# Four units in the first MLP step of a chunked mLSTM kernel, with the opening's instructions in a written order

## The chip, the cores and the metric

The kernel runs on one core of a Trainium2 chip. The core has a matrix engine (PE, with its weight loads shown as PEld), three engines for elementwise work (DVE, ACT, POOL) and SyncE (SP), which here only issues loads. Each engine runs its own instructions in the order in which they stand and waits on semaphores for the others. The metric is the device time of one execution in microseconds; lower is better. Before the change it is 519.04 us, the median of 3 runs (517.11 to 520.46).

## What is computed

An mLSTM layer (a linear recurrence with exponential gates), then an MLP on its output:

```python
for t in range(S):                       # B, H, S, D = 4, 8, 768, 40
    m_new = np.maximum(f[t] + m, i[t])
    f_stab, i_stab = np.exp(f[t] + m - m_new), np.exp(i[t] - m_new)
    C = f_stab * C + i_stab * outer(v[t], k[t])      # per head, 40 x 40
    n = f_stab * n + i_stab * k[t]
    y[t] = sigmoid(o[t]) * (C @ q[t]) / max(|n . q[t]|, 1)
x = y as [3072, 320]
h = x @ w_in                             # 320 -> 2048
out = (h * sigmoid(h)) @ w_out           # 2048 -> 320
```

The weights `w_in` and `w_out` arrive as 64-bit floats; the kernel builds 32-bit floats from their two words.

## The kernel before

The sequence is cut into chunks of 128 steps. A *unit* is one chunk of one batch entry with its 8 heads: 24 units of 128 tokens, unit n being chunk n // 4 of batch entry n % 4. Within a chunk the recurrence is attention with a decay matrix; from one chunk to the next a state `Cm` is carried. A unit passes through these stages (methods of `Unit`):

- loads: `load_qk` (q and k), `load_kvo` (k, v and the output gate), `load_d` (the decay logs, broadcast from a DRAM scratch `LFd`), `load_q`;
- the decay matrix `D`: `exps` on ACT, `mask` on POOL. For units 0 to 2 the logs come over PE instead of by a load: `spread` (tile `pd`), four matmuls for half a unit;
- `products` (PE, scores `ps`), `weigh` (DVE, scores times decay, and the column `vw` for the state), `values` (PE, `po`), `state` (PE, `pu`), `gate` (DVE, normalising and gating into `x`), `carry` (DVE and POOL, `Cm`);
- `xpose` (PE, transposes `x` into `px`), `xhi` (ACT) and `xlo` (DVE), which split the transposed result into a rounded part and a remainder, `xh` and `xl`.

The gates are scans over time on DVE, for 32 rows (batch entries times heads): `gates_scan`, `gates_sub`, `gates_sum`, `gates_top`, then `gates_flip` transposes on PE and `gates_out` stores to `LFd`. Chunk 0 is done first, the other five chunks in one piece in slots 0 to 2 of step 0.

The weights come in 18 parts (`Part`): `i0` to `i7` (256 columns of `w_in`, 256 of its rows), `c0` and `c4` (the last 64 rows for 1024 columns) and `o0` to `o7` (256 rows of `w_out`). A part is loaded (`load`), its magnitude made on ACT (`mag`), its sign and low bits joined by three DVE operations (`join`), and parts of `w_in` are split into `wh` and `wl` (`top` on ACT, `rest` on DVE).

The MLP runs in 8 *steps* of 3 units (384 tokens), each step in 16 *slots* (`fc`, 128 hidden columns). A slot has the first product `mm1` (8 matmuls into a bank `ph`), `glu` (tanh on ACT, then DVE), `halves` (split of the result into two parts, ACT and DVE, from step 1 on) and the second product `mm2` of the slot two earlier (banks `pout`). In step 0 `mm2` takes each product in full 32-bit precision, two matmul records per unit; from step 1 on three matmuls of rounded parts per unit, for which `split_out` splits one part of `w_out` in each of step 1's slots 0 to 7.

Everything is in program order: a list of calls makes the opening (units 0 to 2, parts `i0`, `c0`, `i1`, `o0`), with `spin(k)` putting k idle matmuls (tile `idle`) on PE between them; then step 0's slots carry the attention of units 3 to 5, the remaining weights and late gates by a table `extra`; from step 1 on `piece` spreads each unit's attention over 5 slots (unit 6 begins at slot 0 of step 1) and the loads for a unit two ahead. Buffers come from pools that hand them out in turn: `pb` (10 large ones, for weights, scores' operands and `xh`, `xl`), `pw` (3), and PSUM banks `psO` (3), `psH` (2), `psA` (3).

## Time and profile before

| | |
|---|---|
| median of 3 runs | 519.04 us (517.11 to 520.46) |
| the profiled execution, its own time | 517.62 us |
| its span, first to last instruction | 515.5 us |
| busy: PE, DVE, ACT, POOL | 498.8, 343.7, 267.9, 103.3 us |
| mean granted clock of PE | 0.967 |
| first MLP matmul | 47.67 us |
| first instruction of step 1 (scores of unit 6) | 121.68 us |

All durations are from the one profiled execution. PE's busy time includes idle matmuls (69 records) and, where the clock is below 1, slower matmuls; matmul records overlap, so what a group costs is read from start to start, or from the chain of waits. In a timeline row, the bracket holds the idle time of the engine ahead of it and what ended it. A row of a stretch gives each engine's busy time in it, then PE's granted clock as a share of full speed.

### The profile page before, as it was taken

The page shows a single profiled execution, that of the slowest core. Times are in us where ns is not written, and L with a number is a line of the kernel's source. Part 1 is how long each engine was busy: PE and PEld are TensorE (multiplying, and loading weights), DVE is VectorE, ACT ScalarE, POOL GpSimd, SP SyncE. Part 2 cuts the span into 40 slices and gives each one's busy share as a digit, 9 for nine tenths or more (in the row PEclk, how much of TensorE's full clock was granted, in tenths as well). Part 3 has the DMA queues.
Part 4 walks back from the last instruction along what each step waited for, and adds up shares of the span by engine and source line. Part 5 has one row for each costly group of instructions (what it writes and reads, how often), then busy time and mean ns, then how long its engine had stood idle before and what let it go on. Part 6 is the DMA issues. An engine that isn't in the chain of part 4 may idle for free.

```text
span 515.5 us, 8739 instructions
## 1 busy us (share of the span) xinstructions
PE 498.8 (97%) x3191; PEld 469.0 (91%) x3191; DVE 343.7 (67%) x664; ACT 267.9 (52%) x644; POOL 103.3 (20%) x142
## 2 busy tenths in 40 slices
PE   8899698999999999999999999999999999999996
PEld 4766677888999999999899999999899999999996
DVE  3765869995788767777677767776676666444332
ACT  2433154663665565656556566565655664334332
POOL 1110013330414313321332232233131010000000
PEclk9569698999999999999999999999999999999999
DMA  8861199880633644663464366346346210001001
GB/s 185 276 199 40 51 280 304 264 231 5 178 80 113 185 117 119 174 182 76 152 187 101 113 183 165 90 129 186 101 127 181 67 40 1 0 1 39 0 1 38
DMA packets 38496, 63.96 MB, mean 124 GB/s; under 512 B 3505, under 2 KB 16375, under 8 KB 38455
## 3 DMA queue, kind: packets, MB, share of 16 engines
q1 hardware_dynamic: 34951, 59.38, 41.5%
q10 hardware_dynamic: 3504, 4.03, 2.2%
q8 instruction: 25, 0.41, 0.3%
q14 instruction: 16, 0.13, 0.1%
HBM read 59.37 MB, written 4.03 MB: 123 GB/s over the span
## 4 chain that ended last, share of the span: by engine, by line
PE 82%; DVE 6%; DMA 5%; ACT 4%; issue 2%; SPq 1%; ACTq 1%; DVEq 0%
PE ph L615 31%; PE pout L655 29%; PE po L494 9%; PE ps L460 4%; PE idle L688 2%; PE po L485 2%; PE pu L526 2%; DMA raw<-in_qk_dram 2%; DMA wro<-in_w_out_dram 2%; ACT ob L672 1%; PE px L568 1%; DVE st L376 1%; ACT D L417 1%; DMA qt<-in_qp_dram 1%; DVE th L623 1%
## 5 line engine op out<-in xcount | busy, mean ns | idle before, releaser
L615 PE MATMUL ph<-xh,wh 128*128 128x384 f32 x384 | 138.2, 360 | 0.6 <-ACT xh L580 0.6
L615 PE MATMUL ph<-xl,wh 128*128 128x384 f32 x384 | 130.7, 340 | 0.2 <-DVE xl L586 0.2
L621 ACT ACTIVATE th<-ph 128x384 f32<-128x384 f32 x128 | 62.4, 488 | 113.9 <-PE ph L615 112.3
L655 PE MATMUL pout<-woh,gh 128*128 128x320 f32 x336 | 106.0, 316 | 1.6 <-ACT ob L672 1.0
L635 DVE TENSOR_TENSOR gl<-th,gh 128x384 fp32r<-128x384 f32 x112 | 63.1, 563 | 66.4 <-ACT gh L634 66.4
L655 PE MATMUL pout<-wol,gh 128*128 128x320 f32 x336 | 103.9, 309 | 0.0
L655 PE MATMUL pout<-woh,gl 128*128 128x320 f32 x336 | 103.7, 308 | 0.0
L634 ACT CAST gh<-th 128x384 fp32r<-128x384 f32 x112 | 57.2, 511 | 79.6 <-DVE th L623 79.5
L623 DVE SCALAR_TENSOR_TENSOR th<-th,ph 128x384 f32<-128x384 f32 x112 | 61.4, 548 | 41.8 <-ACT th L621 41.7
L615 PE MATMUL ph<-xh,wl 128*128 128x384 f32 x256 | 87.2, 340 | 0.0
L615 PEld LDWEIGHTS ph<-xh,wh 128*128 128x128 f32 x384 | 73.2, 191 | 2.5 <-ACT xh L580 0.8
L615 PEld LDWEIGHTS ph<-xl,wh 128*128 128x128 f32 x384 | 73.1, 190 | 0.9 <-DVE xl L586 0.4
L655 PEld LDWEIGHTS pout<-woh,gh 128*128 128x128 f32 x336 | 63.0, 188 | 4.2 <-ACT ob L672 4.1
L655 PEld LDWEIGHTS pout<-woh,gl 128*128 128x128 f32 x336 | 63.1, 188 | 0.0
L655 PEld LDWEIGHTS pout<-wol,gh 128*128 128x128 f32 x336 | 63.1, 188 | 0.0
L494 PE MATMUL po<-kvo,D 128*128 128x41 f32 x384 | 51.1, 297 | 6.4 <-issue 4.1
L376 DVE TENSOR_TENSOR st<-raw,st 40x512 fp32r<-40x512 f32 x64 | 52.9, 826 | 6.5 <-ACT st L374 4.6
L494 PEld LDWEIGHTS po<-kvo,D 128*128 128x128 f32 x384 | 49.9, 209 | 7.3 <-issue 4.4
L417 ACT ACTIVATE D<-D,aT 128x128 f32<-128x128 f32 x168 | 53.5, 391 | 0.5
L615 PEld LDWEIGHTS ph<-xh,wl 128*128 128x128 f32 x256 | 48.7, 190 | 0.3 <-DVE wl L246 0.3
L403 POOL TENSOR_SCALAR_AFFINE_SELECT D<-D 128x512 f32<-128x512 f32 x48 | 37.7, 805 | 55.2 <-DMA D<-LFd 32.7
L562 POOL TENSOR_TENSOR Cm<-Cm,ut 120x246 f32<-120x246 f32 (+1 forms) x32 | 22.9, 737 | 95.7 <-DVE ut L561 95.7
(82 smaller groups left out, 572.6 us busy)
## 6 DMA issues: line engine op xcount, KB each, us to landing
raw<-in_qk_dram SPq DMA_DIRECT2D x32, 480.0 KB
kvo<-in_kvo_dram SPq DMA_DIRECT2D x24, 484.0 KB
D<-LFd SPq DMA_DIRECT2D x42, 256.0 KB
wro<-in_w_out_dram SPq DMA_DIRECT2D x8, 640.0 KB
wri<-in_w_in_dram SPq DMA_DIRECT2D x8, 512.0 KB
out_dram<-ob ACTq DMA_DIRECT2D x24, 160.0 KB
qt<-in_qp_dram SPq DMA_DIRECT2D x20, 180.0 KB
lq<-LFd SPq DMA_DIRECT2D x60, 60.0 KB
```

Of the source, the lines that this page charges most:

```text
L376: nc.vector.tensor_tensor(out=t[r0 : r0 + D, :], in0=raw[r0 : r0 + D, :], in1=t[r0 : r0 + D, :].bitcast(F32), op=ALU.subtract,)
L403: nc.gpsimd.affine_select(out=d, in_=d, compare_op=ALU.is_ge, fill=fill, base=0, pattern=[[0, HH], [1, L]], channel_multiplier=-1,)
L417: nc.scalar.activation(d[:, h, :], e[:, h, :], AF.Exp, bias=aT[:, self.c, r + h : r + h + 1])
L460: nc.tensor.matmul(self.ps[hf][:, j, :], k_[:, cs], q_[:, cs], start=True, stop=True)
L494: nc.tensor.matmul(po[:, h, :], self.Dm[:, h, :], self.vt[:, h, :], start=first, stop=(h == H - 1))
L562: nc.gpsimd.tensor_tensor(out=v, in0=v, in1=tv, op=ALU.add)
L615: nc.tensor.matmul(ph, w, x, start=(i == 0), stop=(i == len(ops) - 1))
L621: nc.scalar.activation(th, ph, AF.Tanh, scale=0.5)
L623: nc.vector.scalar_tensor_tensor(out=g, in0=th, scalar=1.0, in1=ph, op0=ALU.add, op1=ALU.mult)
L634: nc.scalar.copy(gh, g)
L635: nc.vector.tensor_tensor(out=gl, in0=g, in1=gh.bitcast(F32), op=ALU.subtract)
L655: nc.tensor.matmul(self.po[t], g[:, ts], w, start=(fc == 0 and i == 0), stop=(last and i == len(ops) - 1),)
```

## The change

1. Step 0 has 4 units (512 tokens), steps 1 to 6 have 3, and step 7 has 2. Units 0 to 3 get their decay logs by `spread`.
2. In step 0 (`Opening`), hidden columns 0 to 3 are done in two halves, kind A for units 0 and 1 and kind B for units 2 and 3 (256 columns wide), and columns 4 to 15 for all four units together (kind J, 512 wide). The second products of the fourth unit lie in the free ends of the banks of units 0 and 1, as 192 and 128 columns.
3. From the first gate scan up to the end of the opening all work follows one written list, `ORDER`, word by word: `mJ4` is the first product of kind J for column 4, `a`, `b`, `n` its tanh, `glu` and second product; `p3` the scores of unit 3, `v`, `w`, `o`, `g`, `u`, `c`, `x`, `h`, `y` its further stages; `Li1`, `Mi1`, `Si1`, `Zi1`, `Ji1`, `Ti1`, `Ri1` the load, magnitude, three joins, `top` and `rest` of part `i1`; `z` one idle matmul, of which there are 30. The list ends with units 0 to 6 done and step 0 complete but for the second products of columns 14 and 15. From step 1 on the old scheme runs, starting with unit 7 (`DONE` 7).
4. Gates: chunks 0, 1 and 2 each in a piece of its own, all within the list; chunks 3 to 5 (`gates_late`) in slots 1 to 7 of step 1.
5. The five pools above become rings: a buffer is given back at a place in the program, and the next taker gets the one that was given back first.

```diff
+NW = 4 * L
+WIDE = 4
-NSTEP = NU // UPS
+NSTEP = 1 + -(-(NU - WIDE) // UPS)
-DONE = 6
+DONE = 7
+ORDER = """
+gs0 qk0 gs1 z gu1 z*5 gs2 gu0 gm0 gt0 z*2 gm1 two z Li0 z Mi0 z Lc0 z*3 p0 gf0 z s0.1 s2.1
+Si0 qk1 z Zi0 e0.1 s0.0 e0.0 Mc0 s1.0 Ji0 e1.0 z k0.1 z*2 s1.1 k0.0 kvo0 Sc0 gt1 r0 Zc0
...
+"""
+    class Ring:
+        def take(self, name, shape, dtype=F32):
+            self.held[name] = k = self.free.popleft()
+            return self.pool.tile(shape, dtype, tag=f"s{k}", name=name)
+        def give(self, *names):
+            for name in names:
+                self.free.append(self.held.pop(name))
...
+    class Opening:
+        SIDE = {"A": (0, 2), "B": (2, 4), "J": (0, 4)}
+        CUT = 512 - DM
+        def mm1(self, kind, fc):
+            u0, u1 = self.SIDE[kind]
+            ph = psH.take(f"ph0{kind}{fc}", [128, 512])[:, : (u1 - u0) * L]
+            first_product(ph, fc, xh0, xl0, slice(u0 * L, u1 * L))
...
+        def mm2(self, kind, fc):
...
+                if u < 3:
+                    nc.tensor.matmul(self.po[u][:, :DM], gs, w, start=(fc == 0), stop=last)
+                else:
+                    nc.tensor.matmul(self.po[0][:, DM:], gs, w[:, :cut], start=False, stop=False)
+                    nc.tensor.matmul(
+                        self.po[1][:, DM : 2 * DM - cut], gs, w[:, cut:], start=False, stop=False
+                    )
...
     class Step:
...
+            self.n0 = WIDE + (j - 1) * UPS
+            self.n = min(UPS, NU - self.n0)
+            self.w = self.n * L
...
+    late = gates_late()
+    rest = (3, NC - 3)
+    extra = {
+        1: dict(end=[lambda: late.scan(*rest)]),
+        3: dict(end=[lambda: late.sub(*rest)]),
+        5: dict(middle=[lambda: late.sum(*rest)], end=[lambda: late.store(*rest)]),
+        7: dict(middle=[lambda: late.top(*rest)],
+                end=[lambda: late.flip(*rest), lambda: big.give("lfi", "lml")]),
+    }
```

Three places show how instructions move. First PE, ahead of the first MLP matmul. Before (`px` are the transposes of a unit, `pu2` unit 2's state product, `ph0_0` the first product of column 0), the rows from unit 1's transposes on, the run of eleven idle matmuls shortened to its first:

```order
L568 MATMUL px1_400<-ident_83,x1_360 128x128 x2
L570 MATMUL px1_400<-ident_83,x1_360 64x128
L571 MATMUL px1_400<-ident_83,x1_360 64x128
L688 LDWEIGHTS G_97
L688 MATMUL idle_110<-G_97 128x512
...
L526 MATMUL pu2_431<-vw2_351,kvo2_161 120x123 x2
L526 MATMUL pu2_431<-vw2_351,kvo2_161 80x82
...
L568 MATMUL px2_436<-ident_83,x2_416 128x128 x2
L570 MATMUL px2_436<-ident_83,x2_416 64x128
L571 MATMUL px2_436<-ident_83,x2_416 64x128
L615 MATMUL ph0_0_486<-xh0_327,wh_89 128x384
```

Now (`ph0A0` is the first product of column 0 for units 0 and 1, `pd3_1` half of unit 3's spread):

```order
L696 MATMUL px1_366<-ident_83,x1_332 128x128 x2
L698 MATMUL px1_366<-ident_83,x1_332 64x128
L699 MATMUL px1_366<-ident_83,x1_332 64x128
L884 LDWEIGHTS G_98
L884 MATMUL idle_116<-G_98 128x512
L491 MATMUL pd3_1_379<-rows_99 128x128 x4
L653 MATMUL pu2_384<-vw2_372,kvo2_324 120x123 x2
L653 MATMUL pu2_384<-vw2_372,kvo2_324 80x82
L653 MATMUL pu1_390<-vw1_322,kvo1_285 120x123 x2
L653 MATMUL pu1_390<-vw1_322,kvo1_285 80x82
L725 MATMUL ph0A0_396<-X_97,wh_89 128x256 x2
...
L620 MATMUL po2_416<-kvo2_324,D2_172 128x41 x8
```

The first product follows unit 1's transposes, with half the width, and unit 2's values (`po2`) come behind it. Where the dots stand are the other six matmuls of `ph0A0`.

Second SP, the loads at the start (`raw` is q and k of a unit, `kvo` its k, v and gate, `wr` a weight part). Before:

```order
L334 DMA raw0_127<-in_qk_dram 40x2x512 x2
L185 DMA wri0_130<-in_w_in_dram 128x2x512
L188 DMA wrc0_132<-in_w_in_dram 64x2x512 x2
L345 DMA kvo0_135<-in_kvo_dram 128x968
L334 DMA raw1_137<-in_qk_dram 40x2x512 x2
L345 DMA kvo1_140<-in_kvo_dram 128x968
L107 DMA LFd_101<-G_97 32x128
L107 DMA LFd_101<-G_97 1x128
L334 DMA raw2_156<-in_qk_dram 40x2x512 x2
L185 DMA wri1_159<-in_w_in_dram 128x2x512
```

Now:

```order
L418 DMA raw0_112<-in_qk_dram 40x2x512 x2
L271 DMA wri0_139<-in_w_in_dram 128x2x512
L274 DMA wrc0_145<-in_w_in_dram 64x2x512 x2
L418 DMA raw1_178<-in_qk_dram 40x2x512 x2
L429 DMA kvo0_219<-in_kvo_dram 128x968
L927 DMA bm_88<-in_bmask_dram 120x123
L429 DMA kvo1_285<-in_kvo_dram 128x968
L271 DMA wri1_294<-in_w_in_dram 128x2x512
L418 DMA raw2_310<-in_qk_dram 40x2x512 x2
L429 DMA kvo2_324<-in_kvo_dram 128x968
```

Unit 1's q and k stand ahead of unit 0's `kvo`, and the gates' store to `LFd` is no longer among these; it follows the load of `kvo3`, for chunk 1 in place of chunk 0.

Third DVE, in the middle of step 0. Before, around the `glu` (L623) of columns 3 to 5:

```order
L623 SCALAR_TENSOR_TENSOR g0_3_638<-th0_3_636,ph0_3_619 128x384
L212 TENSOR_SCALAR wti3_645<-wti3_645 128x512
L215 SCALAR_TENSOR_TENSOR wti3_645<-wri3_589,wti3_645 128x512
L221 SCALAR_TENSOR_TENSOR wti3_645<-wri3_589,wti3_645 128x512
L623 SCALAR_TENSOR_TENSOR g0_4_673<-th0_4_671,ph0_4_659 128x384
L246 TENSOR_TENSOR wl_90<-wti3_645,wh_89 128x2x256
L212 TENSOR_SCALAR wto3_683<-wto3_683 128x640
L215 SCALAR_TENSOR_TENSOR wto3_683<-wro3_640,wto3_683 128x640
L221 SCALAR_TENSOR_TENSOR wo3_698<-wro3_640,wto3_683 128x640
L623 SCALAR_TENSOR_TENSOR g0_5_707<-th0_5_705,ph0_5_689 128x384
```

Now, around the `glu` (L760) of column 4, kind J (`vw4` is unit 4's column for the state, `D4` its weighted scores):

```order
L760 SCALAR_TENSOR_TENSOR g0J4_726<-g0J4_726,ph0J4_702 128x512
L294 TENSOR_SCALAR wti4_697<-wti4_697 128x512
L294 TENSOR_SCALAR wto3_730<-wto3_730 128x640
L301 SCALAR_TENSOR_TENSOR wti4_697<-wri4_538,wti4_697 128x512
L301 SCALAR_TENSOR_TENSOR wto3_730<-wro3_558,wto3_730 128x640
L599 TENSOR_TENSOR D4_495<-ps4_1_571,D4_495 128x512
L314 SCALAR_TENSOR_TENSOR wti4_697<-wri4_538,wti4_697 128x512
L314 SCALAR_TENSOR_TENSOR wo3_795<-wro3_558,wto3_730 128x640
L343 TENSOR_TENSOR wl_90<-wti4_697,wh_89 128x2x256
L294 TENSOR_SCALAR wtc4_782<-wtc4_782 128x512
```

The single operations of two parts and of a unit alternate, and the parts stand further ahead of the columns that use them: `i4` (columns 8 and 9) is joined right behind the `glu` of column 4.

More of the change, by code (lines that the diff above doesn't have):

```diff
@@ L34 @@
 NWT = 3
-DONE = 6
+DONE = 7
+CUT = 10
 TWICE = 2 * UPS
@@ L676, in mlstm_mlp_kernel @@
+            put(n, [(slice(0, DM), self.po[t])], ob)
+            psO.give(f"pout{self.j}_{t}")
+            if not own:
+                big.give(f"ob{n}")
     units = [Unit(n) for n in range(NU)]
     steps = {}
-    def load(n):
-        units[n].load_qk()
-        units[n].load_kvo()
-        units[n].load_d()
-    idle = psH.tile([128, 512], F32, tag="h", name="idle")
+    idle = []
     def spin(k):
+        if not idle:
+            idle.append(psH.take("idle", [128, 512]))
         for _ in range(k):
@@ new lines, in mlstm_mlp_kernel @@
+    UNIT = dict(qk="load_qk", kvo="load_kvo", d="load_d", q="load_q", s="spread", e="shape",
+                k="tri", p="products", v="column", w="weight", t="opened", l="scaled",
+                r="keep", o="values", g="gate", u="state", c="carry", x="xpose", h="xhi", y="xlo")
+    PART = {a + b: f for a, f in dict(
+        L="load", M="mag", S="shift", Z="signs", J="lows", T="top", R="rest").items() for b in "cio"}
+    GATE = dict(gs="scan", gu="sub", gm="sum", gt="top", gf="flip", go="store")
@@ L802, in run @@
+    MLP = {a + b: f for a, f in dict(m="mm1", a="tanh", b="glu", n="mm2").items() for b in "ABJ"}
+    OTHER = dict(z=lambda: spin(1), two=gates_two,
+                 bm=lambda: nc.sync.dma_start(bm, bmask))
+    nc.vector.memset(busy, 1.0)
+    perform(ORDER)
     def run(*calls):
```

675 lines of the change are left out of this document (344 added, 331 removed).

## The prediction

> **What bounds the kernel now.** I read the page's head, then a table of stretches cut where the program changes character: 47.67 us is the first MLP matmul, 121.68 us the start of step 1, and the last row holds slots near the end that have no attention in them.
>
> ```profile
> span 515.5 us, 8739 instructions
> ...
> 0.00:47.67 47.67, 43.25 (x224) 28.81 (x224) 24.48 (x52) 15.22 (x41) 7.08 (x18) 0.79 0.66 189
> 47.67:121.68 74.01, 67.50 (x359) 56.53 (x359) 63.80 (x114) 35.00 (x83) 15.70 (x19) 0.91 0.68 198
> 66.60:121.68 55.08, 52.81 (x288) 43.79 (x287) 47.21 (x83) 28.46 (x67) 14.10 (x17) 0.97 0.84 244
> 121.68:150.00 28.32, 28.32 (x201) 26.93 (x201) 19.77 (x36) 18.20 (x43) 7.13 (x9) 1.00 0.31 85
> 455.02:507.36 52.34, 52.19 (x325) 51.82 (x325) 21.17 (x38) 20.29 (x41) 0.00 (x0) 1.00 0.03 10
> ```
>
> The columns are window, its length, then busy us of PE, PE's weight loads, DVE, ACT and POOL, the granted clock, DMA share and GB/s. From 121.68 us on PE is full at clock 1.00: there the time is the sum of PE's work, and nothing but less work shortens it. Ahead of it PE reads as busy too, but at a clock of 0.79 and 0.91, and partly with idle matmuls. DVE, the next busiest, works 24.48 of the first 47.67 us and 63.80 of the next 74.01.
>
> Next the timeline of PE: where it stood still, and the two marks.
>
> ```profile
> 14.15 0.79 PE L460 MATMUL ps<-raw 40*128 40x128 f32 x2 [1.95 <-DMA raw<-in_qk_dram]
> 47.67 0.44 PE L615 MATMUL ph<-xh,wh 128*128 128x384 f32 x1 [0.57 <-ACT xh L580]
> 56.52 3.61 PE L494 MATMUL po<-kvo,D 128*128 128x41 f32 x16 [4.08 <-issue]
> 83.99 2.09 PE L494 MATMUL po<-kvo,D 128*128 128x41 f32 x16 [2.27 <-DVE D L474]
> 121.68 1.16 PE L460 MATMUL ps<-raw 40*128 40x128 f32 x16
> ```
>
> The granted clock after two of these gaps, in the same columns as above:
>
> ```profile
> 14.00:16.00 2.00, 1.70 (x10) 1.44 (x12) 1.86 (x4) 2.00 (x9) 0.92 (x2) 0.51 0.89 291
> 32.00:34.00 2.00, 2.00 (x7) 0.77 (x7) 1.90 (x3) 0.00 (x0) 0.39 (x1) 0.50 0.95 377
> 34.00:36.00 2.00, 2.00 (x10) 0.95 (x9) 1.90 (x7) 0.55 (x2) 0.00 (x0) 0.87 0.30 94
> 62.00:64.00 2.00, 2.00 (x8) 2.00 (x7) 1.31 (x6) 0.00 (x0) 0.00 (x0) 0.50 0.62 210
> 64.00:66.00 2.00, 2.00 (x6) 1.18 (x5) 1.30 (x2) 1.70 (x3) 1.26 (x2) 0.69 0.97 266
> ```
>
> A gap of 1.95 us was followed by 20 us at half clock, one of 4.08 us by some 9. So the first 121.68 us are bound by a chain that starves PE, and then by the clock that PE loses.
>
> The prices of PE's work, from the chain of waits (start, us, what), are read where the clock was full; a spread is from the timeline, four matmuls of about 0.6 us together.
>
> ```profile
> 35.41 3.38 PE idle L688 x15
> 42.42 0.22 PE px L568 x2
> 42.64 0.11 PE px L570
> 42.75 0.36 PE px L571 x2
> 121.75 1.09 PE ps L460 x16
> 126.05 1.40 PE ph L615 x8
> 127.45 1.61 PE pout L655 x6
> 129.06 0.63 PE po L485 x6
> 129.69 1.75 PE po L494 x16
> 134.26 0.57 PE pu L526 x6
> 136.26 1.33 PE pout L655 x9
> 137.59 0.33 PE px L568 x3
> ...
> 11.22 0.66 PE L392 MATMUL pd<-rows 64*128 64x128 f32 x4
> ```
>
> One unit's attention is thus 1.09 (ps) + 1.75 (po) + 0.57 (pu) + 0.69 (px) = 4.10, and 0.63 more from chunk 1 on. By these prices the opening before holds 69 idle matmuls 15.5, 6 spreads 3.6, six units 25.9, 16 first products 22.4 and 14 second products 22.5: 74 us of useful work and 90 with the idle ones, in 121.68. Some 32 us are lost to waits and half clock.
>
> **The change part by part.** *What leaves the stretch after the opening.* Before, 515.5 - 121.68 = 393.8 us follow the start of step 1. The change takes from it:
> - One unit of the MLP, since 4 units are in step 0 and the last step has 2: 16 slots go from 1.40 + 1.33 to a narrower pair. A 512-column matmul takes 3.38/15 = 0.225 us and a 384-column one 1.40/8 = 0.175, so 256 columns are about 0.123 on the same line (estimate; never below two thirds of 0.175 = 0.117, at most 0.175 if the width didn't matter). Eight make 0.98, and six second products 6 x 1.33/9 = 0.89: 1.87 against 2.73, 16 times: -13.8 (at worst -7.1).
> - Unit 6's attention, now in the order: 1.09 + 0.63 + 1.75 + 0.57 + 0.33 = -4.4.
> - The two second products of step 0 that still run here have 4 units: 4/3 of 1.61 and a little more for the split fourth, 2.17: +1.1.
> - The late gates (three chunks) now run in slots 1 to 7, with three transposes on PE (+0.3) and a second set of DVE scans. Their price is read from these rows of DVE, whose mean is over one scan of 128 and one of 640 columns:
>
> ```profile
> L114 DVE TENSOR_TENSOR_SCAN G<-G 32x128 f32<-32x128 f32 (+1 forms) x2 | 1.9, 974 | 2.8 <-DMA G<-in_ig_dram 2.8
> L623 DVE SCALAR_TENSOR_TENSOR g<-th,ph 128x384 f32<-128x384 f32 x16 | 8.8, 547 | 4.3 <-ACT th L621 4.1
> L474 DVE TENSOR_TENSOR D<-ps,D 128x512 f32<-128x512 f32 x12 | 7.7, 686 | 0.6
> L467 DVE TENSOR_TENSOR vw<-kvo,D 128x328 f32<-128x328 f32 x7 | 3.8, 548 | 0.0
> L511 DVE SCALAR_TENSOR_TENSOR x<-kvo,po 128x320 f32<-128x320 f32 x6 | 2.7, 444 | 2.0 <-ACT kvo L430 2.0
> L514 DVE TENSOR_TENSOR x<-x,den 128x320 f32<-128x320 f32 x6 | 3.0, 493 | 0.2
> L586 DVE TENSOR_TENSOR xl<-px,xh 128x384 fp32r<-128x384 f32 x6 | 3.3, 553 | 4.5 <-ACT xh L580 4.5
> ```
>
>   Two scans of 384 columns at about one mean, and five cheaper passes, make about 4.3 us of DVE. Splitting the operands of unit 8 and half of unit 9 starts five slots earlier than it did for unit 8: about 3.3 more. In 121.68:150.00 DVE was busy 19.77 of 28.32; with 7.6 more it is at 27.4, just short of full, ahead of PE's own stream. I take 2 us of waiting (0, if DVE's slack is well placed; 5, if the burst in slots 3 to 7 is not absorbed).
>
> Sum: 393.8 - 13.8 - 4.4 + 1.1 + 0.3 + 2 = **379.0 us** from the start of step 1 to the end. The end itself (the last 27 second products, then `ob` and its store) keeps its form. Break-even is therefore a step 1 that starts at 515.5 - 379.0 = 136.5 us, 15 us later than before.
>
> *The opening.* By the same prices the new order holds, up to the scores of unit 7: 30 idle matmuls 6.8, 8 spreads 4.8, seven units 28.7 and three times 0.63, 8 half-width first products 7.9, 12 of 512 columns at 8 x 0.225 = 21.6, and 14 second products 30.4: 102 us, 95 of it useful. DVE's work is 24.48 + 63.80 = 88.3 before; one unit more (0.55 + 1.37 + 0.44 + 0.49 + 0.55, and some 0.8 of small rows; its `vw` was already inside) is +3.7; the twelve wide `glu` (0.547 x 512/384 = 0.73) and eight narrow ones (0.37) +2.9; shorter gates about -2: 93 us. Neither engine can end it before 100.
>
> I follow it in three pieces, on the engine that is late in each.
> 1. *To the first product* (`mA0`). It needs only units 0 and 1 transposed, where before all three were; DVE's rows up to the second `xlo` come to 20.8 us by the row durations (weight joins 0.4 to 1.1, units as above). DVE starts near 3.7 us, after the gate load, and waits for the first weight tile as before (about 1.6) and for first products of the scores (I take 2.4): **28.5 us**, against 47.67. Bounds: 26 without the second wait; 41 if DVE is busy 24.48/47.67 of the time as it was.
> 2. *To the first `mB`*. DVE has 14.5 us of rows (unit 2, unit 3, weights i1, o0, i2), PE 12.6 us. I take DVE's with a wait of 1: **15.5 us**. At half clock PE would need 25: the upper bound.
> 3. *To step 1*. PE has 102 - 21 - 12.6 = 68.4 us, DVE about 57. Stepping through the rows, each `glu` and weight that PE needs stands on DVE ahead of PE's place by 0 to 10 us, so PE sets this piece. Lost on top: in 66.60:121.68 PE was idle 2.3 of 55.08 and lost 0.03 of the clock, 7% together; I take 7%: **73.2 us**. Bounds: none; or 26%, as in the whole of 47.67:121.68 (58.5 us of work in 74.01).
>
> Step 1 then starts at 28.5 + 15.5 + 73.2 = 117.2 us, and the span is 117.2 + 379.0 = **496.2 us**.
>
> *The rings* add no instruction. SP waits for the slot that has been free longest, in program order; what is behind a wait is every later load. `kvo3` waits there for the last reader of `kvo0`, with the loads of i2, o1, raw4, o2, i3 behind it; at about 22 us that is in time, as i2 is first used near 35. Late in the order `kvo8` and `kvo7` wait for `pu5` and `pu6`, just before step 1; `kvo7` lands about when the first `tanh` of step 1 is due: nothing, or 2 us if it is late, inside the 7%.
>
> **The rivals.**
> *The clock stays half up to `mB`.* Idle matmuls fall from 69 to 30, and runs of six and fifteen of them stood where the clock came back at 34 to 36 us. For it: 14 to 34 us held half clock through attention work and 12 idle matmuls. Against: the gap that started it was a wait for unit 1's scores, whose load now stands ahead of `kvo0`. Then piece 1 is about 36 (21 us of PE's work, most of it doubled) and piece 2 is 25: step 1 at 134, span 513. [...]
>
> *SP's queue stalls in the middle (slower).* A load that waits for a buffer holds all loads behind it. The SP queue's waits in the first 130 us show the price:
>
> ```profile
> SPq L355 <- PE po L485: 21.8, 2, 20.9
> SPq L107 <- DVE G L133: 19.6, 1, 19.6
> ```
>
> If one such stall of 21 us falls between the second unit's buffers and the weights of columns 4 to 7, the first products wait for it, and half clock follows: 21 + about 9 puts step 1 at 147 and the span at 526. It decides from a stall of some 19 us (with the clock, less). Against it: the gates' chunk 1 is made up front, so neither of the two waits above has its old cause.
>
> *The order packs nearly tight.* 26 + 13.5 + 69 = 108.5, no wait in step 1: span 486.
>
> *It packs no tighter than before:* several small waits put step 1 between 131 and 142, span 510 to 521.
>
> **How the numbers follow.** The profiled run took 517.62 us, 2.1 more than its span; the median of three, 519.04, is 0.27% above it. The forecast is 496.2 + 2.1 = 498.3, times 1.0027: **500 us**. The cases in the same units: tight 489, half clock 516, SP stall 530, no better 514 to 525. Chances: the forecast with its bounds (491 to 508) 0.58; tight 0.12; half clock, whole or in part (508 to 520) 0.17; no better 0.06; SP stall 0.07. The range 489 to 515 leaves out half of "tight", the upper part of the half-clock case and the last two: about 0.2. This kernel's measurement can't tell less than about 1% from no change. Under 513.8: 0.58 + 0.12 + 0.12 of the half-clock case + 0.01 = 0.83; from 513.8 to 524.2: 0.09; above: 0.08.
>
> **What would show it.** In the changed profile: the first matmul of `ph0A` at 26 to 31 us; the first of `ph0B` near 44; the scores of unit 7 near 117; the granted clock at 0.9 or more from there back to `ph0B`, and no PE gap above 2 us in it; after it PE full; the last step's slots at 1.87 us in place of 2.73; 379 us from the scores of unit 7 to the end. Half clock in the rows from 14 to 45 us would show the first rival; a single SP wait of 15 us or more the second. It is wrong if step 1 starts after 136 us, or if 379 is off by more than 5, which would mean that the slots of step 1 wait for DVE.

## The result and the profile after

The changed kernel takes 498.48 us, the median of 4 executions (493.13 to 509.83), where the kernel before, beside it, took 518.08 us (516.65 to 520.46). The ratio is **0.9515, with a 95% interval of 0.9448 to 0.9583**. Executions of one program differ by 10 us or more with the clock that PE is granted: the changed kernel's took 493.13 and 493.27 us at a mean of 0.997 and 0.993, and 503.68 and 509.83 us at 0.969 and 0.956, and the ratio sets the first two against four of the kernel before that all took as long as in its profile (517.62 us at 0.967).

The profiled execution took 493.27 us. The head of its page, and its three stretches up to step 1 with one behind (window, length, busy us of PE, PE's weight loads, DVE, ACT, POOL, then the granted clock, DMA share and GB/s):

```profile
span 491.5 us, 8787 instructions
...
PEclk9999999999988999999999999999999999999999
```

```profile
0.00:25.55 25.55, 23.93 (x168) 16.47 (x171) 20.11 (x50) 15.70 (x45) 5.91 (x16) 1.00 0.90 248
25.55:39.03 13.48, 13.03 (x110) 10.93 (x110) 13.18 (x32) 6.09 (x15) 0.63 (x1) 1.00 1.01 255
39.03:110.21 71.18, 70.99 (x406) 57.58 (x404) 52.20 (x103) 32.69 (x78) 18.46 (x25) 1.00 0.68 199
...
144.00:148.00 4.00, 2.06 (x10) 2.02 (x11) 3.18 (x9) 2.32 (x5) 0.00 (x0) 0.59 0.70 184
```

The clock reads 1.00 in the rows of the whole opening, and PE is busy for 107.95 of its 110.21 us. There is one place left where PE stands still for longer: the digits 8 in the clock's row, at the end of slot 7 of step 1. The timeline of PE, with the marks and that gap:

```profile
13.52 1.16 PE L574 MATMUL ps<-raw 40*128 40x128 f32 x16
...
25.55 0.48 PE L725 MATMUL ph0A<-X,wh 128*128 128x256 f32 x2
...
39.03 0.64 PE L725 MATMUL ph0B<-X,wh 128*128 128x256 f32 x2
...
110.21 1.16 PE L574 MATMUL ps<-raw 40*128 40x128 f32 x16
...
145.94 0.49 PE L208 MATMUL pt<-ident,lfi 32*128 32x32 f32 x3 [3.76 <-DVE lfi L198]
```

Unit 1's scores (13.52) no longer wait, the first product comes at 25.55 in place of 47.67, and step 1 starts at 110.21 in place of 121.68 with one unit more done. The two profiles differ by 24.0 us: 11.5 of them lie ahead of step 1 and 12.5 behind it (381.3 in place of 393.8). The prices of the new pieces, from the chain of waits (start, us, what): the second product of three units, two wide first products, the two pieces of the fourth unit's second product, and a slot of the last step.

```profile
51.21 1.62 PE pout L774 x6
52.83 3.73 PE ph0J L725 x16
...
57.64 0.33 PE pout L776 x2
57.97 0.22 PE pout L777 x2
...
462.16 0.95 PE ph L725 x8
463.10 0.89 PE pout L852 x6
```

What the profile leaves open is why the clock held, how much of the 24 us is clock and how much is work, and what the gap at slot 7 costs. In the experiments "kept the clock" is said of a single execution by its mean granted clock and its time; for the kernels whose profile is quoted the stretch itself is seen.

### The profile page after: what moved, and what is told of

Read it like the earlier page. It is cut to its first block, busy times and chain, and to the rows that moved or that the text cites. A ratio compares the mean times of both kernels' runs of the same rounds, so it can differ in the third digit from the quotient of the medians.

```text
span 491.5 us, 8787 instructions
## 1 busy us (share of the span) xinstructions
PE 480.5 (98%) x3205; PEld 453.2 (92%) x3208; DVE 338.1 (69%) x686; ACT 267.1 (54%) x653; POOL 102.2 (21%) x141
## 4 chain that ended last, share of the span: by engine, by line
PE 78%; DVE 9%; DMA 6%; ACT 5%; issue 2%; ACTq 1%; SPq 0%; POOL 0%; DVEq 0%
PE ph L725 27%; PE pout L852 25%; PE po L620 6%; PE ph0J L725 4%; PE pout L774 4%; PE ps L574 3%; PE po L611 2%; DMA wri<-in_w_in_dram 2%; DVE st L460 2%; PE pu L653 2%; ACT D L518 2%; PE idle L884 1%; DMA kvo<-in_kvo_dram 1%; ACT ob L730 1%; PE px L696 1%
## 5 line engine op out<-in xcount | busy, mean ns | idle before, releaser
L852 PE MATMUL pout<-woh,g 128*128 128x320 f32 x640 | 161.6, 312 | 1.2 <-ACT ob L730 0.8
L725 PE MATMUL ph<-xh,wh 128*128 128x384 f32 (+1 forms) x336 | 116.7, 347 | 0.0
L852 PEld LDWEIGHTS pout<-woh,g 128*128 128x128 f32 x640 | 112.4, 189 | 3.6 <-ACT ob L730 3.4
L725 PE MATMUL ph<-xl,wh 128*128 128x384 f32 (+1 forms) x336 | 111.4, 332 | 0.0
L838 DVE TENSOR_TENSOR g<-th,g 128x384 fp32r<-128x384 f32 (+1 forms) x112 | 60.6, 541 | 65.7 <-ACT g L837 65.7
L852 PE MATMUL pout<-wol,g 128*128 128x320 f32 x320 | 99.1, 310 | 0.0
L837 ACT CAST g<-th 128x384 fp32r<-128x384 f32 (+1 forms) x112 | 55.5, 496 | 76.9 <-DVE th L827 76.9
L827 DVE SCALAR_TENSOR_TENSOR th<-th,ph 128x384 f32<-128x384 f32 (+1 forms) x112 | 59.2, 529 | 38.8 <-ACT th L826 38.7
L725 PE MATMUL ph<-xh,wl 128*128 128x384 f32 (+1 forms) x224 | 74.5, 332 | 0.0
L852 PEld LDWEIGHTS pout<-wol,g 128*128 128x128 f32 x320 | 60.5, 189 | 0.0
L503 POOL TENSOR_SCALAR_AFFINE_SELECT D<-D 128x512 f32<-128x512 f32 x48 | 37.9, 810 | 34.8 <-ACT D L518 21.1
```

The lines of the kernel that those rows point to most:

```text
L503: nc.gpsimd.affine_select(out=d, in_=d, compare_op=ALU.is_ge, fill=fill, base=0, pattern=[[0, HH], [1, L]], channel_multiplier=-1,)
L725: nc.tensor.matmul(ph, w, x, start=(i == 0), stop=(i == len(ops) - 1))
L827: nc.vector.scalar_tensor_tensor(out=th, in0=th, scalar=1.0, in1=ph, op0=ALU.add, op1=ALU.mult)
L837: nc.scalar.copy(gh, g)
L838: nc.vector.tensor_tensor(out=gl, in0=g, in1=gh.bitcast(F32), op=ALU.subtract)
L852: nc.tensor.matmul(self.po[t], g[:, ts], w, start=(fc == 0 and i == 0), stop=(last and i == len(ops) - 1),)
```

## How much of the gain is the clock

**The old kernel with one load moved.** If unit 1's late q and k had cost the old kernel its clock, one line should return it.

```diff
-    u0.load_kvo()
     u1.load_qk()
+    u0.load_kvo()
```

> The kernel before the change with one edit: the load of unit 1's q and k stands ahead of unit 0's kvo, as in the changed kernel; everything else, the 69 idle matmuls too, as before. Theory (the load order only removes the gap; the first product then waits for unit 2's chain on DVE): the 1.95 us gap goes or shrinks below 1 us, the clock from 14 to 34 us is over 0.8 in place of 0.50, but DVE's rows, and the wait for unit 0's kvo one load later, still set the first product: 44 to 47 us in place of 47.67, span 511 to 515. Rival (half the gain of the change is the clock that the one load cost): the first product comes 10 us or more earlier, span 500 to 506. Other rival (the gap moves to the next operand, unit 0's kvo, and the clock falls all the same): span 514 to 518.

The median was 519.64 us (510.08 to 521.29, 4 executions), beside 519.22 for the old kernel. One of the four kept the clock (mean 0.983, the others 0.964 to 0.967), and so had 3 of 8 of the old kernel in the same session (0.981 to 0.987, the others 0.962 to 0.967): the edit decides nothing. But the profiled execution is the one that kept it, and so shows what the old order does at full clock (the stretches up to the first product and up to step 1, then PE's two longest gaps and the start of step 1):

```profile
0.00:37.31 37.31, 34.75 (x219) 22.05 (x224) 24.01 (x52) 15.24 (x41) 7.73 (x18) 1.00 0.82 242
37.31:113.82 76.51, 69.15 (x358) 57.98 (x358) 63.68 (x114) 34.99 (x83) 15.97 (x19) 0.89 0.65 191
```

```profile
46.16 3.61 PE L494 MATMUL po<-kvo,D 128*128 128x41 f32 x16 [4.07 <-issue]
...
74.50 3.42 PE L494 MATMUL po<-kvo,D 128*128 128x41 f32 x16 [3.07 <-DVE D L474]
...
113.82 1.16 PE L460 MATMUL ps<-raw 40*128 40x128 f32 x16
```

The first product comes 10.4 us earlier than in the profile before, step 1 7.9 earlier, and the span is 507.7. Between this and the changed kernel's 491.5 lie 16.2 us at the same clock in the first 37 us: 3.6 ahead of step 1 (113.82 to 110.21), although one unit more is done there, and 12.6 behind it. So about 8 of the 24 us between the two profiles are the clock of the opening, and 16 the change itself: mostly the work that no longer lies behind step 1, and 3.6 us ahead of it, where the old kernel's half clock behind its later gaps (0.89 in the row above) is still inside. No run separates the written order from the fourth unit. The theory had the first product at 44 to 47, held back by DVE; at full clock it comes at 37.31, as the rival had it, and the span lies between the two.

**The old kernel, fed with idle matmuls.** 37 idle matmuls where PE starved (`feed(k)` puts k of them into a bank of their own):

```diff
-    spin(1)
+    spin(10)
     u1.products()
...
-        2: dict(first=[u[3].values, u[3].state], ...
+        2: dict(first=[lambda: feed(16), u[3].values, u[3].state], ...
-        7: dict(first=[u[4].values, u[4].state], ...
+        7: dict(first=[lambda: feed(12), u[4].values, u[4].state], ...
```

> The kernel before the change with idle matmuls where PE starved: 9 more ahead of unit 1's scores (the gap of 1.95 us), 16 ahead of unit 3's values in slot 2 of step 0 (the gap of 4.08 us), 12 ahead of unit 4's values in slot 7 (the gap of 2.27 us). Nothing else is changed; it does the same work in the old order. It asks how much of the gain is the clock alone. Theory (of the 24 us between the two profiles some 8 are the half clock from 14 to 34 us, which the old kernel's load order brings in most executions, some 2 to 4 the half clock behind the later gaps, and the rest is less work after step 1 and denser packing): every execution starts step 1 at 108 to 115 us and the span is 502 to 510. Rival A (nearly all the gain is clock): span under 498. Rival B (the added idle matmuls, 37 x 0.22 = 8 us, land on PE's path, or DVE sets the pace): span 510 to 518, no better than before.

The median was 511.83 us (509.86 to 512.94), and all 10 executions kept the clock (mean 0.988 to 0.993), where 4 of the 13 of the old kernel beside it did (510.63 to 510.94). Against these four and a fifth at 516.05, whose mean clock was lower (0.969 against 0.986 and 0.987), the ratio is 0.9995 (0.9958 to 1.0032); against the four alone the fed kernel is 1.1 us longer. The feed makes the good case regular and no better. Its timeline says why:

```profile
54.06 0.41 PE L568 MATMUL px<-ident,x 128*128 128x128 f32 x2 [0.98 <-DVE x L514]
...
74.84 0.87 PE L485 MATMUL po<-Cm,qt 120*128 120x123 f32 x6 [3.75 <-DVE D L474]
...
114.79 1.16 PE L460 MATMUL ps<-raw 40*128 40x128 f32 x16
```

The gap of 4.07 us is filled, but PE still waits 3.75 us for DVE's `D` of unit 4, and step 1 starts at 114.79. The times lie at the theory's upper edge and a little over it. Idle matmuls alone bring about 8 us to the old kernel's usual execution; the other 16 need the change.

## What the load order has to do with it

**Unit 1's q and k behind unit 0's `kvo`**, as in the old order, within the new one:

```diff
-Si0 qk1 z Zi0 ... kvo0 Sc0
+Si0 z Zi0 ... kvo0 qk1 Sc0
```

> The changed kernel with one word of its list moved: the load of unit 1's q and k stands behind unit 0's kvo, as in the kernel before, in place of ahead of it. Theory (the load order and the short way to the first product keep PE supplied, and a PE that isn't starved keeps its clock): PE waits for unit 1's scores again, some 1 to 2 us near 13.5 us, as it did for 1.95 us before; half clock follows for part of the 12 us behind it, and the first product, at 25.55 us in the changed kernel, comes 4 to 12 us later; all else as it is, so the span goes from 491.5 to 495 to 504. Rival A (the number of idle matmuls and the density of the order decide the clock, not this load): no gap over 1 us, clock 1.00 in the opening, span within 2 us of 491.5. Rival B (half clock, once begun, lasts up to the first product of kind B as in the first rival of the prediction): span 505 to 513.

493.19 us (492.90 to 493.41), and all 4 executions kept the clock (mean 0.991 to 0.997). Against the executions of the old kernel in the session that kept it (509.98 to 513.05), the ratio is 0.967 (0.9647 to 0.9693); the old kernel's mean clock was 0.981 to 0.987 there, and in the profile above with 0.983 the first 37.31 us read 1.00, so this is like against like. The span is 491.5 as for the changed kernel, and unit 1's scores start without a wait, behind a longest gap of 0.40 us:

```profile
12.55 0.66 PE L491 MATMUL pd<-rows 64*128 64x128 f32 x4 [0.40 <-ACT D L518]
...
13.67 1.16 PE L574 MATMUL ps<-raw 40*128 40x128 f32 x16
```

The theory's gap didn't come; rival A is right. The prediction rested its full clock on this load, and that reason is wrong.

**Unit 1's q and k one step earlier still**, ahead of the first weight tile:

```diff
-Li0 z Mi0 z Lc0 ... Si0 qk1 z Zi0
+qk1 Li0 z Mi0 z Lc0 ... Si0 z Zi0
```

> The changed kernel with unit 1's q and k one step earlier still in SP's queue, ahead of the first weight tile. It doubles the suspected cause: the first weight tile lands later. Theory (that tile's landing, through ACT, decides whether PE starves near 10 us): ACT's magnitude of part i0 starts at 9 us or later, half clock in the opening in nearly every execution, 499 to 504 us. Rival (the load order has no part in it): as the changed kernel, 493 in about half of the executions or more.

508.19 us (506.15 to 513.24): none of 12 executions kept the clock (mean 0.953 to 0.970). The path is seen on ACT and PE:

```profile
11.19 0.66 ACT L286 ACTIVATE wti<-wri 128x512 f32<-128x512 f32 x1 [4.70 <-DMA wri<-in_w_in_dram]
11.75 2.16 ACT L518 ACTIVATE D<-pd,aT 128x128 f32<-128x128 f32 x8
```

```profile
12.94 1.11 PE L491 MATMUL pd<-rows 64*128 64x128 f32 x4 [3.49 <-ACT D L518]
...
41.22 0.77 PE L725 MATMUL ph0A<-X,wh 128*128 128x256 f32 x2
...
130.32 1.16 PE L574 MATMUL ps<-raw 40*128 40x128 f32 x16
```

```profile
48.00:50.00 2.00, 2.00 (x17) 1.78 (x16) 1.49 (x4) 0.00 (x0) 0.00 (x0) 0.50 0.99 281
```

ACT waits for the first weight tile up to 11.19 us (in the changed kernel's profile up to 7.76), the exponentials of the decay matrix stand behind that on ACT, and PE waits 3.49 us for the bank which they read. The four matmuls `pd` behind that wait take 1.11 us, where four take 0.66 at full clock, and half clock lasts up to 51.7 us (the row of 51.00:52.00 has 0.67, the next 1.00). It cost more than the theory's 499 to 504: in this execution, one of the two slowest of the twelve, step 1 starts at 130.32, 20 us late.

**The exponentials ahead of that wait.** If ACT's wait is what starves PE, taking four exponentials out from behind it should help.

```diff
-Li0 z Mi0 z Lc0 ... Si0 qk1 z Zi0 e0.1 s0.0
+Li0 z*2 Lc0 ... qk1 z e0.1 Mi0 Si0 Zi0 s0.0
```

> The changed kernel with one move on ACT: the magnitude of part i0 (which waits for the first weight tile) stands behind the first four exponentials of unit 0's decay matrix in place of ahead of them; its first join on DVE moves behind it. In the profile that had half clock in the opening, ACT waited 2.76 us for that tile up to 9.28 us, the exponentials stood behind it, and PE then waited 0.77 us for the bank that they read. Theory (a load that lands late stalls ACT, ACT stalls the spreads on PE, and that gap is what costs the clock): every execution keeps the clock in the opening, 491 to 494.5, though the join comes some 1 us later. Rival (the gap has another cause, such as the scores' load): as many executions with half clock as before the move, about half of them at 500 to 510.

498.72 us (493.84 to 504.21): 3 of 6 executions kept the clock (mean 0.991 to 0.993, the others 0.969), as in the changed kernel. The rival is right: in the usual order another thing than this wait decides. With the changed kernel and two below, in which only the late gates are moved, that makes 9 of 18 executions that kept it.

## What the idle matmuls do

**Without 16 of the 30** (those behind unit 0's first scores; idle matmuls compute nothing):

```diff
-... p0 gf0 z s0.1 s2.1 Si0 qk1 z Zi0 ... k1.0 z*2 s2.0 z*2 p1 ...
+... p0 gf0 s0.1 s2.1 Si0 qk1 Zi0 ... k1.0 s2.0 p1 ...
```

> The changed kernel with 16 of its 30 idle matmuls, those behind the first scores of unit 0, left out; the 14 ahead of them stay. Idle matmuls compute nothing. Theory (PE is the limit from about 13 us on and each idle matmul is on its path, 0.22 us): where PE has no other work a gap takes the place of one idle matmul, elsewhere the time is saved: span 488 to 491.5, clock 1.00 still, gaps under 1 us. Rival (the idle matmuls are what holds the clock at 1.00): half clock in part of 10 to 40 us, and the span 500 to 513.

500.58 us (499.57 to 502.00): none of 4 executions kept the clock (mean 0.968 to 0.973). The timeline of PE and its clock:

```profile
10.06 0.66 PE L491 MATMUL pd<-rows 64*128 64x128 f32 x4 [0.94 <-ACT D L518]
11.09 1.07 PE L491 MATMUL pd<-rows 64*128 64x128 f32 x4 [0.38 <-ACT D L518]
...
33.57 0.77 PE L725 MATMUL ph0A<-X,wh 128*128 128x256 f32 x2
```

```profile
10.00:12.00 2.00, 1.56 (x8) 1.40 (x8) 1.26 (x3) 1.78 (x7) 1.28 (x2) 0.79 1.09 241
12.00:14.00 2.00, 1.16 (x8) 1.00 (x8) 2.00 (x5) 2.00 (x9) 0.66 (x1) 0.50 1.02 308
14.00:34.00 20.00, 20.00 (x104) 17.75 (x102) 13.77 (x33) 8.65 (x25) 2.92 (x4) 0.50 0.90 277
```

3.6 us of idle work are saved, and the time is 7.4 us longer than the 493.2 of the changed kernel at full clock. The rival holds, at the lower end of its range and a little under it (spans of 497.7 to 500.2); the theory, by which PE keeps its clock once it has work, falls.

**With 16 more** (46):

```diff
-... p0 gf0 z s0.1 s2.1 Si0 qk1 z Zi0 ... k1.0 z*2 s2.0 z*2 p1 ...
+... p0 gf0 z*2 s0.1 s2.1 Si0 qk1 z*2 Zi0 ... k1.0 z*4 s2.0 z*4 p1 ...
```

> The changed kernel with each idle matmul behind the first scores of unit 0 doubled: 46 in place of 30, 16 more at 0.225 us, 3.6 us if all lie on the path. Theory (from about 13 us on PE is the limit and idle matmuls are on its path except where they fill a wait): the first product of kind A 1 to 3 us after 25.55 us, clock 1.00 as it is, span 492.5 to 495. Rival (the idle matmuls fill waits that PE has anyway): span 491 to 492. Other rival (some of the lost clock of single executions is due to too few of them): the same best time, but no execution over 496.

495.77 us (494.93 to 495.96): all 4 executions kept the clock (mean 0.991 to 0.997). The span is 493.8, 2.3 us more than the changed kernel's, for 3.6 us of idle work; the first product comes at 27.84. The theory's price and the second rival's "no execution over 496" are both met; its "same best time" isn't (494.93 against 493.13). An idle matmul here costs about 0.14 us each time. That it buys a better chance of the 10 us is likely, but 4 of 4 against 9 of 18 doesn't show it.

## What the halves bring

Columns 0 to 3 in one product for all four units:

```diff
-... y1 mA0 ... aA0 ... bA0 mA1 ... mB0 aB0 ... bB0 mB1 ...
+... y1 ... mJ0 aJ0 ... bJ0 mJ1 ...
...
-            for u in sorted(range(u0, u1), key=lambda u: -(u > 2)):
+            for u in sorted(range(u0, u1), key=lambda u: -(u > 2 and fc > 0)):
```

The second edit puts the fourth unit's second product of column 0 behind those of the other three, which open the banks that it shares.

> The changed kernel without halves: columns 0 to 3 too are done for all four units in one product, at the places where kind B stood; the four products of kind A, with their tanh, glu and second products, are left out and their units come with kind J. The same sums are computed. Theory (the halves only fill the time in which units 2 and 3 are not ready yet): from 25.55 to 39.03 us PE did two A products and one A second product, some 3.5 us, which now come later; all four A products and second products together are 4 x (0.98 + 1.1) = 8.3 us of PE, now done as part of wider ones at a little less cost. PE waits for unit 3 instead, a gap of 2 to 4 us ahead of the first product; step 1 starts 2 to 6 us later than 110.21 and the span is 494 to 498, 500 if the gap brings half clock. Rival (a quarter or more of the gain is due to the halves): the wait and the clock together cost over 8 us, span 500 to 510. Second rival (the narrow products are dearer than their share): span within 1.5 us of 491.5.

Three of four executions took 496.99 to 498.90 us (mean clock 0.986 to 0.990), the fourth 516.02 (0.945). The profiled span is 496.2, 4.7 more than with halves. Its timeline:

```profile
36.42 0.66 PE L680 MATMUL px<-ident,x 128*128 128x128 f32 x2 [1.68 <-DVE x L624]
...
39.85 1.22 PE L709 MATMUL ph0J<-X,wh 128*128 128x512 f32 x2
...
116.37 1.16 PE L558 MATMUL ps<-raw 40*128 40x128 f32 x16
```

Without the narrow products PE waits for DVE (0.72, 0.67 and 1.68 us around 30 to 36), loses its clock from 32.6 to 42.9 us (the 16 matmuls `po` from 31.81 on take 2.92 us, where the 16 from 15.63 on take 1.87), and step 1 starts 6.2 us late; 1.5 of it comes back behind. As the theory said, the halves fill the time in which units 2 and 3 are not ready. They are 5 of the 16 us, half clock included (4.7 in the spans).

## The gap at slot 7

On DVE the rows ahead of the flip in the changed kernel are:

```profile
143.69 0.43 DVE L637 SCALAR_TENSOR_TENSOR x<-kvo,po 128x320 f32<-128x320 f32 x1
...
144.79 0.55 DVE L827 SCALAR_TENSOR_TENSOR th<-th,ph 128x384 f32<-128x384 f32 x1
145.26 0.54 DVE L198 SCALAR_TENSOR_TENSOR lfi<-lfi,lml 32x384 f32<-32x384 f32 x1
```

The last operation of the gates stands behind unit 7's gate and slot 7's `glu`, so PE, which reaches the flip at 142, stands for 3.76 us. Four kernels move it.

**All late gates to slots 8 to 15:**

```diff
-        1: scan, 3: sub, 5: sum and store, 7: top (middle), flip (end)
+        8: scan, 10: sub, 12: sum and store, 13: top (middle), 15: flip (first)
```

> The changed kernel with the late gates (chunks 3 to 5) moved from slots 1 to 7 of step 1 to slots 8 to 15: scan in 8, sub in 10, sum and store in 12, top in 13, the transposes (flip) ahead of slot 15's first product. In slots 0 to 7 DVE also splits w_out (split_out), in 8 to 15 it does not. Theory (at the end of slot 7 PE stands still 3.76 us for the gates on DVE and then runs at half clock for about 5 us, because two sets of work for DVE fall on the same slots): the gap and the half clock at 144 to 150 us both go, span 485 to 487. Rival A (DVE is behind anyway, so PE waits elsewhere in step 1): span 489 to 492. Rival B (the store to the DRAM scratch then comes too late for the decay logs of the first units of chunk 3): a new wait in step 2, span 492 to 500.

**Only the flip, to slot 10:**

```diff
-        7: dict(middle=[lambda: late.top(*rest)],
-                end=[lambda: late.flip(*rest), lambda: big.give("lfi", "lml")]),
+        7: dict(middle=[lambda: late.top(*rest)]),
+        10: dict(first=[lambda: late.flip(*rest), lambda: big.give("lfi", "lml")]),
```

> The changed kernel with only the transposes of the late gates (flip) moved, from the end of slot 7 of step 1 to ahead of slot 10's first product; the gates on DVE stay in slots 1 to 7. Theory (PE, which runs in order, stands still only because the flip is asked for before DVE has made it; DVE's work as such delays nobody else): the gap of 3.76 us and the half clock behind it go, span 485.5 to 488, as much as with all the gates later. Rival (DVE's crowded slots cost PE elsewhere as well): half of that or less, span 488.5 to 491.5, and more from moving the gates than from moving the flip.

The executions that kept the clock (mean 0.993 to 0.997) took 490.70 and 491.47 us with all gates later, and 490.79 and 491.32 with the flip later: some 2 us better than 493.2, which is what the rivals of both said; only "more from moving the gates than from moving the flip" didn't come. From the start of step 1 to the end it is 378.5 (501.8 - 123.26) and 378.6 us (489.5 - 110.92), against 381.3. In both the flip now waits elsewhere, 1.34 us for `xl` each time; with the flip in slot 10:

```profile
152.30 0.37 PE L208 MATMUL pt<-ident,lfi 32*128 32x32 f32 x3 [1.34 <-DVE xl L710]
```

The transposes of a unit (`px`, read by `xl`) and those of the flip (`pt`) come from the same ring, `psA`; `xl` is made in slot 9 (and 14), so the bank is just being read: a new wait, from the choice of slot.

The profile with the gates later is of an execution that lost its clock in the opening, and so shows the first rival of the prediction in the new order (marks of PE, then the clock):

```profile
11.03 0.66 PE L491 MATMUL pd<-rows 64*128 64x128 f32 x4 [0.77 <-ACT D L518]
...
37.84 0.77 PE L725 MATMUL ph0A<-X,wh 128*128 128x256 f32 x2
...
52.81 0.65 PE L725 MATMUL ph0B<-X,wh 128*128 128x256 f32 x2
...
123.26 1.16 PE L574 MATMUL ps<-raw 40*128 40x128 f32 x16
```

```profile
14.00:36.00 22.00, 21.77 (x101) 17.33 (x103) 13.65 (x31) 9.25 (x29) 3.52 (x5) 0.50 0.77 241
...
38.00:40.00 2.00, 2.00 (x12) 2.00 (x11) 1.29 (x2) 0.07 (x1) 0.00 (x0) 0.50 0.97 181
40.00:42.00 2.00, 1.95 (x16) 1.79 (x17) 0.10 (x1) 1.87 (x6) 0.06 (x1) 0.93 1.08 215
```

Piece 1 takes 37.8 us in place of 25.6; piece 2 takes 15.0, hardly more than 13.5, because the clock is back shortly after 40 us.

**The flip in slot 12**, clear of `xl`, with unit 1's q and k behind unit 0's `kvo` as above:

```diff
-        7: dict(middle=[lambda: late.top(*rest)],
-                end=[lambda: late.flip(*rest), lambda: big.give("lfi", "lml")]),
+        7: dict(middle=[lambda: late.top(*rest)]),
+        12: dict(first=[lambda: late.flip(*rest), lambda: big.give("lfi", "lml")]),
```

> Two edits of the changed kernel together: unit 1's q and k behind unit 0's kvo in SP's queue, and the transposes of the late gates (flip) ahead of slot 12's first product in place of the end of slot 7. The flip at slot 10 waited 1.34 us for xl, the last reader of a bank that the transposes reuse; xl is made in slots 4, 9 and 14, so slot 12 is clear of it. Theory (the flip's place was the only loss in step 1, and the first weight tile lands earlier when unit 1's q and k do not load beside it, so PE doesn't starve near 10 us): step 1 starts at 110 us in every execution, 375 to 377.5 us follow it, no PE gap over 1 us behind 20 us, span 485 to 488, no execution over 496. Rival (DVE is behind PE in slots 7 to 12 whatever the flip does): the wait turns up on another tile, span 488.5 to 490.

488.73 us, the median of 7 executions; the five that kept the clock (mean 0.999 and 1.000) took 487.80 to 488.93, spans 486.0 to 487.1, and two took 498.99 (0.973) and 503.19 (0.968). The first of these is the profiled one. From step 1 on its trace shows no flip wait and 376.2 us (497.2 - 120.96), as expected; one wait of 0.80 us, for `st` on DVE, is left. The gap at slot 7 and its half clock had cost 5 us. The other half of the theory fell: two executions lost the clock. And the trace of one, PE around the drop, has no gap ahead of it longer than 0.28 us, behind PE's first instruction:

```profile
7.45 1.11 PE L491 MATMUL pd<-rows 64*128 64x128 f32 x8 [0.28 <-DVE rows L234]
...
9.93 0.83 PE L884 MATMUL idle<-G 128*128 128x512 bf16 x3
10.70 1.11 PE L491 MATMUL pd<-rows 64*128 64x128 f32 x4
```

```profile
10.00:12.00 2.00, 2.00 (x8) 1.20 (x9) 0.75 (x3) 2.00 (x8) 0.63 (x1) 0.65 1.11 272
...
12.00:36.00 24.00, 24.00 (x111) 18.63 (x110) 14.16 (x32) 9.92 (x30) 3.51 (x5) 0.50 0.76 234
36.00:38.00 2.00, 2.00 (x12) 2.00 (x12) 1.99 (x5) 0.00 (x0) 0.00 (x0) 0.52 0.95 188
38.00:40.00 2.00, 2.00 (x20) 2.00 (x20) 0.00 (x0) 1.61 (x6) 0.00 (x0) 1.00 1.05 238
```

The same four matmuls `pd` take 0.66 us at full clock and 1.11 from 10.70 on. From 7.45 us on PE reads as busy throughout. Up to step 1 this kernel is the same program as the one above with q and k behind `kvo`, whose trace kept the clock behind a gap of 0.40 us. So neither the order, nor the number of idle matmuls, nor the length of the gaps decides alone.

**The same with 9 more idle matmuls between the scores of units 0 and 1:**

```diff
-p0 gf0 z s0.1 ... e1.0 z k0.1 z*2 s1.1 ... k1.0 z*2 s2.0 z*2 p1
+p0 gf0 z*2 s0.1 ... e1.0 z*2 k0.1 z*4 s1.1 ... k1.0 z*4 s2.0 z*4 p1
```

> The kernel with unit 1's q and k behind unit 0's kvo and the flip ahead of slot 12 (the two edits together, as run before), and with the 9 idle matmuls between unit 0's scores and unit 1's scores doubled to 18; the other 21 are as they were. The profile of the two edits alone had half clock from 10.7 us on without a PE gap over 0.3 us ahead of it, so a gap as such is not what decides. Theory (what decides is how much PE has to do from 7 to 14 us, and idle matmuls count as work): no execution with half clock in the opening, every one within 487.5 to 491 (486.0 to 487.1 of span in the good executions of the two edits, and up to 9 x 0.225 = 2.0 us more). Rival (the number of idle matmuls there has no part in it, only chance): two or three of about ten executions at 498 to 504 again.

490.27 us, the median of 6; five took 489.47 to 490.78 (mean clock 0.998 to 1.000) and one 505.89 (0.966). So 9 more idle matmuls there are no protection: the theory fell at that one execution, though the five lie where it said. From step 1 on it is 376.6 us (488.7 - 112.06), the flip without a wait again. The ratio to the old kernel, 0.9533 (0.942 to 0.9646), and 0.9501 (0.9403 to 0.9599) with 30 idle matmuls, says too much: among the old kernel's executions in it stand 517.55 in the one, 517.02 and 517.93 in the other, which had lost the clock. At full clock on both sides it is 490.07 against a single 510.52 us, 0.960, and 488.57 against 511.10, 0.956. So the two are 3.1 and 4.6 us better than the changed kernel's 493.2; the flip's slot brings that, and the 9 idle matmuls cost 1.5. At full clock the kernel with 30 idle matmuls and the flip in slot 12 is the fastest of all here.

## Why the prediction was right, and where it was not

*The time.* Forecast 500 us, measured 498.48 as a median and 493.27 for the profiled execution, for which the forecast was 498.3; the span is 491.5 against 496.2. That the median comes within 1.5 us of the forecast is partly luck: two executions with half clock lift it, and at full clock the forecast was 5 us too long. The four pieces, measured against predicted: 25.55 against 28.5, 13.48 against 15.5, 71.18 against 73.2, 381.3 against 379.0.

*Piece 1* was too long by 3.0, outside its bound of 26. DVE ended unit 1's `xlo` at 25.03 and was idle for 5.4 of 25.55 us, 2.9 of it ahead of the gate load and 2.6 behind it. So all three terms of DVE's sum were oversized: the start (3.7 us, measured 2.9), the waits of 1.6 and 2.4 us on top of the rows (4.0 together, measured 2.6, the longest 0.88) and the rows (20.8, measured some 19.5). PE's own stream, 23.93 busy, was as late as DVE: the first product follows `pu` and not a wait.

*Piece 2* was too long by 2.0: PE and DVE were both full, 13.03 and 13.18 of 13.48. The wait of 1 us didn't come, and DVE's rows, sized at 14.5, took 13.2.

*Piece 3* came as reasoned: PE sets it, 70.99 of 71.18 busy. Its work was 71.0 against the 68.4 of the sum (4% more; a wide product is 3.73/2 = 1.87 and not 1.80), but the loss of 7% on top didn't come. In sum 2.0 too long.

*Behind step 1* the terms of work fit: 0.95 + 0.89 = 1.84 for a slot of the last step (1.87), 1.62 + 0.33 + 0.22 = 2.17 for the wide second product (2.17). The missized term is the 2 us of DVE wait: the late gates cost 5, its upper bound, in one place: a gap of 3.76 us and half clock behind it. With the flip in slot 12, 376.2 and 376.6 us are left, where the sum without that term says 377.0.

*The break-even* wasn't reached: step 1 starts at 123.26 us with half clock (the gates later) and at 130.32 in the worst trace (q and k earliest), where 136.5 was the limit.

*The clock.* The forecast was right that it held in the profiled execution, and wrong on why. The step that failed is the one against the first rival: "the gap that started it was a wait for unit 1's scores, whose load now stands ahead of `kvo0`". Put back behind `kvo0`, nothing is lost; put still earlier, every execution loses the clock; and in the old kernel the same move left 1 of 4 executions at full clock, beside 3 of 8 without it. The rival, at 0.17, has the marks of 2 of the 4 executions of the changed kernel (mean clock 0.969 and 0.956 in place of 0.993 and 0.997), and these two lift the median to 498.48. Of its price of 513, piece 1 at 36 fits (37.8 and 36.5 us in two traces with half clock), and piece 2 at 25 doesn't (15.0 and 13.7), since the clock was back soon after the first products. The spans seen are 501.8 in the first of these traces, 501.9 and 508.0 in the changed kernel's own two executions, which have no trace, and 511.4 where half clock lasted up to 51.7 us.

*The other rivals.* No stall of SP held up PE: in the opening PE had no wait over 0.4 us behind its first instruction. The longest wait of SP there, 14.7 us for a buffer of `qt`, ended at 98.55 us and cost PE nothing (30.00 of 30.00 us busy from 80 to 110); that is just under the 15 us which the prediction had named as the sign of this rival, so the sign alone would not have told it. "Nearly tight" (108.5 and 486) came closest for the opening, 110.21, but the flip took back 5 us.

*The range* held both the median and the profiled execution, and its lower end needed the tight case: the best executions of the changed kernel are at 493, of the mended one at 488.

## What stays open

What lets the clock drop between 10 and 14 us isn't settled. PE's gaps ahead of or at the drop were 1.95 us in the kernel before, 3.49 with the q and k load earliest, 0.94 and 0.38 without the 16 idle matmuls, 0.77 with the gates later and 0.28 with the flip in slot 12; gaps of 0.40 (flip in slot 10) and 0.57 (the old kernel with the load moved) were not followed by it. Clear are two ends: 0 of 12 executions with the load earliest, and 10 of 10 of the old kernel fed with 37 idle matmuls, where that kernel itself kept the clock in 11 of 53 executions of all sessions. Between them lie 9 of 18 (changed order), 14 of 17 (q and k behind `kvo`, three kernels), 4 of 4 (16 more idle matmuls) and 0 of 4 (16 fewer), numbers too small to rank; they also come from several sessions, in which the old kernel itself kept the clock in 0 of 4, 3 of 8, 4 of 13, 3 of 17 and 1 of 11. That more work on PE between 7 and 14 us helps fits the four counts that differ in idle matmuls or in PE's wait, but not the executions of one program that fall to both sides; it is argued, not shown.

## What to carry to other kernels

Behind step 1 PE was full (55.00 of 55.00 us busy from 430 to 485 in the changed kernel), and there the work taken out counted in full and could be priced from single rows: with the flip in slot 12, 376.2 and 376.6 us are left of the 393.8, where the sum without a wait says 377.0. Before a gain is put down to an order, look at the clock of both profiles: here a third of the difference was a clock that the old kernel keeps in one execution out of five. A step that an engine has to wait for in order (here three small transposes) goes to a slot where its producer has finished and its bank has long been read; that was worth 5 us, and in two other places the step still waited 1.34 us and brought 2.7.
